# Softcap attention, gated MLP and gated convolution on one core: the product of the values with the reciprocals is issued two ticks later behind the sums

## The chip, the core and the metric

One core of a Trainium2 chip runs the whole program in one launch. The metric is device time in microseconds, the median of the runs shown; lower is better. TensorE (PE in the profile) multiplies matrices, VectorE (DVE) and ScalarE (ACT) work element by element, GpSimd (POOL) clears tiles and issues the DMAs of the normalization, and SyncE (SP) issues the other DMAs.

## The reference

Three stages follow one another. The change lies in the first, the attention with capped scores over 2 batches and 12 heads of 448 positions and 64 columns:

```python
scores = scale * np.matmul(q, k.transpose(0, 1, 3, 2))
scores = cap * np.tanh(scores / cap)
scores = scores - np.max(scores, axis=-1, keepdims=True)
attn = np.exp(scores)
attn = attn / (np.sum(attn, axis=-1, keepdims=True) + 1e-09)
return np.matmul(attn, v)
```

Its output, regrouped to x of 2 x 448 x 768, goes into a gated MLP (a matrix product with w_in, gelu, a layer norm, a product over positions, a gate, w_out and a residual), and that into a gated convolution (w2_in, relu, three taps, sigmoid, w2_out).

## The kernel before

The heads are worked in pairs, twelve of them: pair N belongs to batch N // 6 and to rows N % 6 of X, the tile in which the attention's output stands for the next stage. A loop over R (L452) takes two steps of R per pair, one per half. In an even step, `scores` (L308) issues the twelve products of the first half, in an odd one the nine of the second; ScalarE then takes the tanh of the half (L317) and the exponential (L318), and since the PSUM tile of the scores exists once, the next half's products wait for that tanh. `values` (L344) follows one step behind, from R = 13 on two: products of the exponentials with V into the PSUM tile pv, and products with ones into the PSUM tile su, which are the sums of the softmax. Beside them VectorE prepares K and Q of later pairs (L92, L95, L262, L263) and decodes pieces of the weights w_in (L135 to L152, tile f), and at R = 13, 17, 21, 23 and 25 TensorE gets products of the next stage that read finished rows of X (`FILL`, tile mo).

When both halves of a pair are through, `norm` (L377) copies the sums to se on VectorE (L389), which frees su, and the values to E on ScalarE (L390). Every second pair it normalizes both together. GpSimd sends the sums to a narrow tile ss (L397). Three pieces of work are put off with `later(k, fn)`, which runs fn k ticks on; a step of R has two ticks. `s1` adds a guard to the sums, takes the reciprocal (L406, L407) and has GpSimd send it to DRAM as d (L410). `s1b` has GpSimd send it back, broadcast to all rows, as rb (L416, four DMAs). `s2` multiplies E by rb on VectorE (L423), copies the product to X on ScalarE (L94 in `split`) and puts the rest of it beside it with a subtraction on VectorE (L95). There are six such normalizations: of the pairs 0 and 1, 2 and 3, 4 and 5, 6 and 7, 8 and 9, and of pair 10. `norm` is reached for them at R = 4, 8, 12, 17, 21 and 23, between the two ticks of the step. Pair 11 goes another way, without DMAs (`norm_pe`).

What sets the order: a scheduler places each instruction when it is issued, and `pin(last)` puts an instruction behind a given one. L406 and L423 are pinned behind `lastv`, the last marked instruction on VectorE, which is the end of a preparation of Q or K, of a gelu, or of an `s2` (its subtraction); the copy to X is pinned behind `lasta`, the last exponential. Functions that fall due in one tick run in the order in which they were put off.

Of the kernel before, what the change touches and what calls it, by code (L numbers as in the profile page):

```python
# [48 lines left out]
def stages(  # L49
# [23 lines left out]
    def pin(last):  # L73
        return tc.issue_after(last[0].ins) if last[0] is not None else ExitStack()
# [3 lines left out]
    def later(k, fn):  # L78
        due.setdefault(now[0] + k, []).append(fn)
# [10 lines left out]
    def split(raw, hi, lo, hi_eng="v"):  # L90
        if hi_eng == "v":
            V.tensor_copy(hi, raw)  # L92
        else:
            A.activation(hi, raw, AF.Copy)  # L94
        return V.tensor_tensor(out=lo, in0=raw, in1=f(hi), op=ALU.subtract)  # L95
# [123 lines left out]
    def attention(att, psa):  # L219
# [124 lines left out]
        def values(N, half):  # L344
# [28 lines left out]
            if half:  # L373
                del acc[N]
                norm(N, ps, su)

        def norm(N, ps, su):  # L377
            b, p = divmod(N, NPAIR)
            if N >= B * NPAIR - NFAST:
                return norm_pe(N, ps, su)  # L380

            j = N % 2
            if j == 0:
                pairs[:] = (
                    att.tile([P, 2, S // 2], F32, tag="se", name="se", bufs=2),
                    att.tile([P, 2, S], F32, tag="E", name="E", bufs=3),
                )
            se, e = pairs
            V.tensor_copy(se[:, j], su)  # L389
            A.activation(e[:, j], ps, AF.Copy)  # L390
            last = N == B * NPAIR - NFAST - 1
            if j == 0 and not last:
                return

            m = j + 1
            ss = att.tile([P, 14], F32, tag="ss", name="ss", bufs=2)[:, : 7 * m]
            G.dma_start(ss, se[::32, :m])  # L397
            rb = att.tile([P, 2, S], F32, tag="rb", name="rb", bufs=2)
            eb, rb = e[:, :m], rb[:, :m]

            ds = []


            def s1():
                with pin(lastv):
                    V.tensor_scalar(out=ss, in0=ss, scalar1=guard, scalar2=None, op0=ALU.add)  # L406
                V.reciprocal(out=ss, in_=ss)  # L407
                ds.append(dr.tile([2, 2, m, S // 2], F32, tag=f"d{m}", name="d"))
                d = ds[0]
                G.dma_start(d.rearrange("h f j (p c) -> (h f j p) c", c=7 * m), ss)  # L410

            def s1b():
                (d,) = ds
                for h in range(2):
                    for i in range(m):
                        G.dma_start(  # L416
                            rb[h * D : (h + 1) * D, i].rearrange("p (f c) -> p f c", f=2),
                            d[h, :, i].partition_broadcast(D),
                        )

            def s2():
                with pin(lastv):
                    V.tensor_tensor(out=eb, in0=eb, in1=rb, op=ALU.mult)  # L423
                with pin(lasta):
                    lastv[0] = split(eb, X[:, 0, p - j : p + 1, b], X[:, 1, p - j : p + 1, b], "a")

            later(3, s1)
            later(4, s1b)
            later(11, s2)

        def norm_pe(N, ps, su):

            b, p = divmod(N, NPAIR)
            r = att.tile([P, 2, S // 2], F32, tag="se", name="r", bufs=2)[:, 0]
            V.tensor_scalar(out=r, in0=su, scalar1=guard, scalar2=None, op0=ALU.add)
            V.reciprocal(out=r, in_=r)
            e = att.tile([P, 2, S], F32, tag="E", name="E", bufs=3)[:, 0]
            A.activation(e, ps, AF.Copy)
            rp = psa.tile([P, 512], F32, tag="su", name="rp", bufs=1)[:, :S]
            for c in range(2):  # L440
                for h in range(2):
                    lastr[0] = T.matmul(
                        rp[h * D : (h + 1) * D, c * S // 2 : (c + 1) * S // 2],
                        lhsT=sel[:, 2 * h + c], rhs=r, start=True, stop=True,
                    )
            V.tensor_tensor(out=e, in0=e, in1=rp, op=ALU.mult)
            split(e, X[:, 0, p, b], X[:, 1, p, b], "a")
# [450 lines left out]
```

## Time and profile before

| | us |
|---|---|
| runs shown | 344.87, 345.75, 345.68 |
| median of the runs | 345.68 |
| span of the profiled execution | 344.2 |
| the profiled execution's own time | not given beside its span |
| TensorE busy | 329.7 (96% of the span) |
| VectorE busy | 252.6 (73%) |
| ScalarE busy | 224.9 (65%) |
| GpSimd busy | 35.2 (10%) |

The span goes from the first to the last instruction of one execution; a run's time takes in what lies around it. Times in the rows are microseconds from the start of the span. A bracket at the end of a row gives how long the engine stood idle before it and what ended that idle time. DMA-issuing instructions are not counted as busy.

### The profile page before, as it was taken

Reading aid. Unit: us, or ns where it says so; the run is one execution under the profiler, and the core shown is the slowest. Engines: PE = TensorE matmul, PEld = TensorE weight load, DVE = VectorE, ACT = ScalarE, POOL = GpSimd, SP = SyncE. Lnnn points to the kernel's source line nnn. Section 1 sums busy time; section 2 is a strip of 40 time slices with the busy share of each in tenths; the row PEclk is TensorE's granted clock in tenths of the full one; section 3 lists DMA queues with packets and bytes.
Section 4 is the critical chain, followed back from the end, with each engine's and each line's share of the span. In section 5 each row is a group of like instructions: output and inputs, shape, how many; then the busy total and the mean of one; then the engine's idle time right before and its main releaser. Section 6 shows DMA issues by size and latency. Waiting matters only on the chain.

```text
span 344.2 us, 5129 instructions
## 1 busy us (share of the span) xinstructions
PE 329.7 (96%) x1814; PEld 251.5 (73%) x1814; DVE 252.6 (73%) x493; ACT 224.9 (65%) x361; POOL 35.2 (10%) x71
## 2 busy tenths in 40 slices
PE   6999999979999999999999999999999999999992
PEld 4544444534446567898899999999999999999991
DVE  4487878769686367997999679997995999970000
ACT  1799889978798236585775564465784988863110
POOL 3000300403030323110121000000000000000000
PEclk9899999998999999999999999999999999999997
DMA  6857754854421124313213384002284122013111
GB/s 178 264 165 237 196 158 142 206 140 124 84 68 43 48 90 126 113 46 93 62 62 122 109 256 170 2 0 59 65 274 155 32 61 91 3 54 132 58 55 33
DMA packets 18698, 37.67 MB, mean 109 GB/s; under 512 B 3980, under 2 KB 9160, under 8 KB 18664
## 3 DMA queue, kind: packets, MB, share of 16 engines
q1 hardware_dynamic: 16952, 34.41, 32.3%
q0 software_dynamic: 1472, 2.61, 3.2%
q8 instruction: 16, 0.26, 0.3%
q10 hardware_dynamic: 240, 0.23, 0.3%
q14 instruction: 18, 0.15, 0.1%
HBM read 34.41 MB, written 2.79 MB: 108 GB/s over the span
## 4 chain that ended last, share of the span: by engine, by line
PE 76%; issue 11%; DMA 5%; DVE 3%; POOL 2%; SPq 1%; ACT 0%; DVEq 0%; POOLq 0%; ACTq 0%
PE mo L98 17%; PE mo L99 17%; PE mo L100 17%; PE pv L305 5%; PE sc L305 4%; PE mo L603 3%; PE mo L605 3%; PE mo L604 3%; PE mo L305 3%; PE su L305 2%; DMA d<-ss 2%; DMA rb<-d 2%; POOL rb L416 2%; DMA ss<-se 1%; PE idle L305 1%
## 5 line engine op out<-in xcount | busy, mean ns | idle before, releaser
L98 PE MATMUL mo<-X,WI 128*128 128x448 f32 x126 | 46.1, 367 | 0.0
L99 PE MATMUL mo<-X,WI 128*128 128x448 f32 x126 | 45.9, 366 | 0.0
L100 PE MATMUL mo<-X,WI 128*128 128x448 f32 x126 | 45.9, 365 | 0.0
L305 PE MATMUL pv<-raw,V 128*64 128x448 f32 (+1 forms) x168 | 45.1, 579 | 0.0
L305 PE MATMUL sc<-Q,K 64*128 64x448 f32 (+1 forms) x252 | 39.3, 395 | 5.3 <-ACT raw L317 3.5
L318 ACT ACTIVATE raw<-raw,one 128x1792 f32<-128x1792 f32 (+3 forms) x26 | 39.1, 1503 | 0.6
L305 PEld LDWEIGHTS sc<-Q,K 64*128 64x128 f32 (+1 forms) x252 | 24.5, 188 | 20.2 <-issue 6.7
L130 ACT ACTIVATE f<-f 128x512 f32<-128x512 f32 (+3 forms) x57 | 31.0, 545 | 10.7 <-DMA f<-in_w_out_dram 5.8
L317 ACT ACTIVATE raw<-sc 128x1792 f32<-128x1792 f32 (+1 forms) x22 | 32.4, 1475 | 7.8 <-PE sc L305 7.5
L140 DVE SCALAR_TENSOR_TENSOR f<-f 128x512 uint32<-128x512 uint32 (+3 forms) x57 | 30.3, 542 | 9.0 <-ACT f L133 8.5
L99 PE MATMUL mo<-HG,W 128*128 128x448 f32 x96 | 34.8, 365 | 0.0
L100 PE MATMUL mo<-HG,W 128*128 128x448 f32 x96 | 34.7, 365 | 0.0
L98 PE MATMUL mo<-HG,W 128*128 128x448 f32 x96 | 34.1, 365 | 0.0
L143 DVE SCALAR_TENSOR_TENSOR f<-f 128x512 uint32<-128x512 uint32 (+3 forms) x57 | 30.7, 546 | 0.3
L305 PEld LDWEIGHTS pv<-raw,V 128*64 128x64 f32 (+1 forms) x168 | 11.9, 145 | 22.0 <-issue 18.5
L98 PEld LDWEIGHTS mo<-X,WI 128*128 128x128 f32 x126 | 23.6, 188 | 2.4 <-DVE u L179 0.4
L100 PEld LDWEIGHTS mo<-X,WI 128*128 128x128 f32 x126 | 23.6, 188 | 2.0
L99 PEld LDWEIGHTS mo<-X,WI 128*128 128x128 f32 x126 | 23.7, 188 | 2.0
L783 ACT ACTIVATE o<-mo 128x448 f32<-128x448 f32 x12 | 6.3, 543 | 26.1 <-PE mo L100 23.0
L133 ACT ACTIVATE f<-f 128x256 uint32<-128x256 uint32 (+2 forms) x44 | 22.6, 515 | 0.0
L99 PEld LDWEIGHTS mo<-HG,W 128*128 128x128 f32 x96 | 18.0, 188 | 1.4
L98 PEld LDWEIGHTS mo<-HG,W 128*128 128x128 f32 x96 | 18.0, 188 | 1.4
(141 smaller groups left out, 650.3 us busy)
## 6 DMA issues: line engine op xcount, KB each, us to landing
f<-in_w_in_dram SPq DMA_DIRECT2D x24, 512.0 KB, 4.4
f<-in_w_out_dram SPq DMA_DIRECT2D x24, 256.0 KB, 4.2
V<-in_vL_dram SPq DMA_DIRECT2D x12, 256.0 KB, 3.7
f<-in_w_out_dram SPq DMA_DIRECT2D x8, 384.0 KB, 3.1
qr<-in_qT_dram SPq DMA_DIRECT2D x24, 112.0 KB, 3.1
out_dram<-o SPq DMA_DIRECT2D x12, 224.0 KB, 1.9
rb<-d POOLq DMA_DIRECT2D x22, 112.0 KB, 3.8
kr<-in_kT_dram SPq DMA_DIRECT2D x11, 112.0 KB, 3.1
```

The costliest lines, as they stand in the source:

```text
L98: matmul(ps, lhsT=whi, rhs=xhi, start=start, stop=False)
L99: matmul(ps, lhsT=whi, rhs=xlo, start=False, stop=False)
L100: matmul(ps, lhsT=wlo, rhs=xhi, start=False, stop=stop)
L130: A.activation(f(h), f(h), AF.Copy, scale=2.0**-112)
L133: A.activation(l, l, AF.Copy, scale=0.93 * 2.0**-29)
L140: V.scalar_tensor_tensor(out=l, in0=h, scalar=3, in1=l, op0=ALU.logical_shift_left, op1=ALU.bitwise_or)
L143: V.scalar_tensor_tensor(out=l, in0=h, scalar=0x80000000, in1=l, op0=ALU.bitwise_and, op1=ALU.bitwise_or)
L305: lastm[0] = T.matmul(*args, **kw)
L317: A.activation(raw[:, t], ps[:, t, :S], AF.Tanh, **sc)
L318: lasta[0] = A.activation(raw[:, t], raw[:, t], AF.Exp, scale=capc)
L603: T.matmul(ps, lhsT=xs(0, k), rhs=WI[1][:, 0, k], start=k == 0, stop=False)
L604: T.matmul(ps, lhsT=xs(0, k), rhs=WI[1][:, 1, k], start=False, stop=False)
```

## The change

One number changes, the count of ticks from a normalization's issue to its `s2`:

```diff
             later(3, s1)
             later(4, s1b)
-            later(11, s2)
+            later(13, s2)
```

It moves instructions on VectorE, ScalarE, GpSimd and SP; TensorE's stand as before.

On VectorE, at the first normalization's product (E_282, rb_363) and the second one's sums (ss_525), K0, Q and the decoding of the weights (f64, WI0) around them:

```order
 L95 TENSOR_TENSOR K0_87<-kr0_89,K0_87 128x512
+L406 TENSOR_SCALAR ss_525<-ss_525,one_72 128x14
+L135 TENSOR_SCALAR f64_530<-f64_530 128x512
 L423 TENSOR_TENSOR E_282<-E_282,rb_363 128x896
 L263 SCALAR_TENSOR_TENSOR Q_585<-qr_483,one_72,Q_585 128x448
 L143 SCALAR_TENSOR_TENSOR f64_452<-f64_452 128x512
+L407 RECIPROCAL ss_525<-ss_525 128x14
 L149 CAST WI0_76<-f64_452 128x512
```

The two instructions on ss_525, which stood behind the subtraction of X from E_282 one step later, now stand on both sides of the product.

On ScalarE, at the second normalization's copy to X (E_442), with the tanh and exponential of one half (raw), the decoding (f64) and the copy of the values (pv):

```order
+L130 ACTIVATE f64_696<-f64_696 128x512
+L317 ACTIVATE raw_776<-sc_775 128x1344
+L318 ACTIVATE raw_776<-raw_776,one_72 128x1344
 L94 ACTIVATE X_75<-E_442 128x2x448
-L130 ACTIVATE f64_696<-f64_696 128x512
-L317 ACTIVATE raw_779<-sc_778 128x1344
-L390 ACTIVATE E_806<-pv_762 128x448
-L318 ACTIVATE raw_779<-raw_779,one_72 128x1344
 L130 ACTIVATE f64_724<-f64_724 128x512
+L390 ACTIVATE E_806<-pv_759 128x448
```

The copy to X stands behind the tanh and the exponential of its step, where it stood ahead of them.

On VectorE, at the second normalization's product (E_442, rb_527) and the third one's sums (ss_691):

```order
 L95 TENSOR_TENSOR K0_87<-kr0_89,K0_87 128x512
+L406 TENSOR_SCALAR ss_691<-ss_691,one_72 128x14
+L135 TENSOR_SCALAR f64_696<-f64_696 128x512
+L423 TENSOR_TENSOR E_442<-E_442,rb_527 128x896
 L263 SCALAR_TENSOR_TENSOR Q_750<-qr_649,one_72,Q_750 128x448
-L143 SCALAR_TENSOR_TENSOR f64_618<-f64_618 128x512
-L423 TENSOR_TENSOR E_442<-E_442,rb_527 128x896
-L149 CAST WI1_77<-f64_618 128x512
-L152 TENSOR_TENSOR WI1_77<-f64_618,WI1_77 128x512
+L143 SCALAR_TENSOR_TENSOR f64_615<-f64_615 128x512
+L407 RECIPROCAL ss_691<-ss_691 128x14
```

The product stands two operations earlier on VectorE, and the third normalization's sums stand ahead of it. On GpSimd the four DMAs of the fifth normalization's rb now stand ahead of the sixth one's ss, which they followed.

## Rows read from the trace of the kernel before

**Rows 1.** the page's head: span, and TensorE's busy time with its share.

```profile
span 344.2 us, 5129 instructions
...
PE 329.7 (96%) x1814; PEld 251.5 (73%) x1814; DVE 252.6 (73%) x493; ACT 224.9 (65%) x361; POOL 35.2 (10%) x71
```

**Rows 2.** the page's chain that ended last, shares of the span by engine.

```profile
PE 76%; issue 11%; DMA 5%; DVE 3%; POOL 2%; SPq 1%; ACT 0%; DVEq 0%; POOLq 0%; ACTq 0%
```

**Rows 3.** timeline of PE: start, duration, instructions, [idle before <- releaser].

```profile
57.69 1.48 PE L305 MATMUL sc<-Q,K 64*128 64x448 f32 x12 [0.23 <-ACT raw L317]
...
66.54 1.72 PE L305 MATMUL pv<-raw,V 128*64 128x448 f32 x8
...
68.71 1.69 PE L305 MATMUL sc<-Q,K 64*128 64x448 f32 x9
...
72.18 0.96 PE L305 MATMUL su<-raw,ones 128*32 128x224 f32 x16
75.33 1.50 PE L305 MATMUL sc<-Q,K 64*128 64x448 f32 x12 [2.19 <-ACT raw L317]
76.76 3.09 PE L305 MATMUL pv<-raw,V 128*64 128x448 f32 x8
...
80.57 1.69 PE L305 MATMUL sc<-Q,K 64*128 64x448 f32 x9
...
97.64 0.58 PE L305 MATMUL su<-sm,ones 128*32 128x224 f32 x8 [0.39 <-DVE se L389]
```

**Rows 4.** timeline of ACT, around its longest idle.

```profile
72.60 0.95 ACT L94 ACTIVATE X<-E 128x896 fp32r<-128x896 f32 x1 [2.46 <-DVE E L423]
...
74.02 1.27 ACT L317 ACTIVATE raw<-sc 128x1344 f32<-128x1344 f32 x1
```

**Rows 5.** timeline of DVE, 49 to 79 us.

```profile
49.44 0.69 DVE L95 TENSOR_TENSOR K<-kr,K 128x512 fp32r<-128x512 f32 x1
...
56.78 1.08 DVE L95 TENSOR_TENSOR X<-E,X 128x896 fp32r<-128x896 f32 x1
57.78 0.23 DVE L406 TENSOR_SCALAR ss<-ss,one 128x14 f32<-128x14 f32 x1
...
62.40 0.38 DVE L389 COPY se<-su 128x224 f32<-128x224 f32 x1
...
66.87 0.70 DVE L143 SCALAR_TENSOR_TENSOR f<-f 128x512 uint32<-128x512 uint32 x1
71.47 1.09 DVE L423 TENSOR_TENSOR E<-E,rb 128x896 f32<-128x896 f32 x1 [3.90 <-DMA rb<-d]
...
78.59 0.38 DVE L389 COPY se<-su 128x224 f32<-128x224 f32 x1
```

**Rows 6.** the tile f to 130 us: duration ns min/median/max of L135.

```profile
L135 DVE TENSOR_SCALAR f<-f x13: 178/422/427, 10.1 to 96.3; 128x512 uint32<-128x512 uint32 x12, 128x24 uint32<-128x24 uint32 x1
```

**Rows 7.** timeline of POOL's DMA issues in the same stretch.

```profile
46.48 0.73 POOL L397 DMA_DIRECT2D ss<-se  x1 [5.33 <-DVE se L389]
...
60.32 0.57 POOL L410 DMA_DIRECT2D d<-ss  x1 [13.10 <-DVE ss L407]
...
62.74 2.54 POOL L416 DMA_DIRECT2D rb<-d  x4 [1.86 <-DMA d<-ss]
```

**Rows 8.** landings of ss issued at 46.48 and at 65.27, of rb issued from 62.74.

```profile
DMA to landing us min/median/max: 4.0/4.0/4.0
...
DMA to landing us min/median/max: 6.3/6.3/6.3
...
DMA to landing us min/median/max: 6.0/6.6/6.8
```

**Rows 9.** stretches: busy by engine (instructions), PEclk, DMA share, GB/s.

```profile
60.00:65.00 5.00, 4.80 (x35) 2.81 (x33) 4.31 (x9) 4.77 (x5) 2.82 (x5) 1.00 0.65 174
...
76.76:78.50 1.74, 1.74 (x8) 0.68 (x8) 1.74 (x5) 1.74 (x3) 0.00 (x0) 0.56 0.15 52
...
130.00:150.00 20.00, 20.00 (x93) 17.26 (x93) 17.73 (x35) 13.00 (x27) 5.53 (x6) 1.00 0.34 103
```

## The prediction

> **What bounds the kernel now.** I read the page first: span 344.2 us, TensorE busy 329.7 of it, 96% [rows 1]. Anything that pays must therefore take out one of TensorE's few idle stretches, or a stretch in which it is busy but slow. The chain of waits says where to look: beside 76% TensorE it holds 5% DMA, 3% VectorE and 2% GpSimd [rows 2], and the lines behind these are those of the normalization, L397 to L423. So the next view is TensorE's timeline in the attention stage. The step whose scores begin at 75.33 waits 2.19 us with nothing running, and it waits for ScalarE's tanh, L317 [rows 3]. ScalarE's timeline shows why that tanh is late: the engine stood idle 2.46 us before the copy of X (L94) at 72.60, waiting for VectorE's product L423; only behind that copy comes the tanh at 74.02 [rows 4]. VectorE stood idle 3.90 us before that product, waiting for the broadcast reciprocals rb [rows 5]. GpSimd's issues close the loop: this second normalization's sums went out at 46.48 and landed 4.0 us later [rows 7, 8], but its DMA of the reciprocals, d, left at 60.32 after 13.10 us of waiting for L407 [rows 7], and rb, issued from 62.74, landed up to 6.8 us after its issue [rows 7, 8]. The sums lay ready from 50.5; L406 took them up at 57.78, right behind the subtraction of X at 56.78 of the normalization before [rows 5].
>
> That is an order, not a shortage. A product (s2) and the next normalization's sums (s1), four steps of R apart, fall due in one tick: 2R+1+11 for the one, 2(R+4)+1+3 for the other. The product is taken first and sets lastv to its subtraction, and the sums are then pinned behind it.
>
> **What the change does.** With 13 the product falls due one tick pair later, behind those sums. The first order piece shows it: the sums' L406 (ss_525) moves from behind X's subtraction to before L423, L407 follows three operations later, and L423 itself stays between the same K and Q operations. The sums of the third normalization and of the fifth move ahead in the same way (ss_691 in the third piece); the fourth's keep their place behind the third's product, because five steps lie between them. No instruction is added or removed, TensorE's order is unchanged, and GpSimd's changes at one place, the fifth rb before the sixth ss.
>
> *Second normalization.* VectorE reaches L406 when K's subtraction of 49.44 is through, about 50.0, and now waits for the sums until 46.48 + 4.0 = 50.5: a new wait of 0.4. L423 (1.09), Q and L143 (0.60 to 0.70 each, [rows 5]) and L407 follow, so d leaves near 53.8 instead of 60.32. Keeping the distance from d to rb of the trace, 62.74 - 60.32 = 2.42, and the largest landing, 6.8 after an issue that ends 1.9 later, rb is there by 53.8 + 2.4 + 1.9 + 6.8 = 64.9. Its product now comes at about 67.3 (below). The 3.90 us wait disappears with 2.4 us to spare.
>
> *What TensorE gets.* (a) X's copy of the first normalization stands one exponential later on ScalarE, so the tanh before the scores at 57.69 is no longer behind it: 0.23 us [rows 3]. (b) The second copy moves in the same way behind the tanh and exponential of its step (second order piece), and its product is early anyway. TensorE's sums of 72.18 end 0.96 later; ScalarE's tanh, free from 70.14 (72.60 less the idle 2.46), is done before 72.2. The 2.19 us go. (c) Behind the idle time the eight products at 76.76 took 3.09 us instead of 1.72 at 66.54, at a granted clock of 0.56 of full speed, so mostly at 1.2 GHz [rows 3, 9]. From the eight products to the next nine it is 80.57 - 76.76 = 3.81 against 68.71 - 66.54 = 2.17: 1.64 us, which return if the clock stays up. (d) At 97.64 TensorE waits 0.39 for VectorE's copy of the sums, se, out of PSUM [rows 3]. VectorE was late there from waiting for the third rb, and that wait goes the same way: with its sums taken up at 66.8 (below), d leaves near 70.0 and rb is there by 81.1 at the distances above, while its product stands thirteenth behind the se copy of 75.2, twelve operations between them at 7.12 / 13 = 0.55 us each on average, near 82. Sum: 0.23 + 2.19 + 1.64 + 0.39 = **4.45 us**.
>
> The Trainium skill speaks against (c): TensorE: Matmul & The Clock Gate, "A second HAM failure mode: psum-queue depth-cycling", reports a kernel whose short idles between groups of products were enough for the clock to swing. By that rule the sum is 2.81, since short idles remain. The trace does not bear it out: from 60 to 65 us TensorE was busy 4.80 of 5.00 and the clock stayed at 1.00, which is 2.4 GHz [rows 9]. I take the 1.64.
>
> *What it costs.* VectorE gets no more work, but its work up to the next se copy is put in another order, and that copy is what TensorE's next sums wait for. I bound it by rows. The third normalization's se is copied at 62.40 [rows 5]; GpSimd, no longer issuing rb until 65.28 (62.74 + 2.54, [rows 7]), sends the sums at about 62.8. The landing is not known there; its ends are the 4.0 of 46.48 and the 6.3 of 65.27 [rows 8]. I take 4.0, because the later one shared the queue with four rb that are now gone: 66.8. VectorE could use them at about 66.2, 0.6 before the 66.87 at which L143 stands [rows 5]. So it idles 0.6, and L423 starts at 67.3. From L423 to the se copy the trace has 78.59 - 71.47 = 7.12 without a gap [rows 5]. Operations overlap by some 0.08: the 1.08 of 56.78 is followed after 1.00. So the change takes out X's subtraction (1.00), one L406 (0.23 - 0.08 = 0.15, [rows 5]) and two L135 (0.42 - 0.08 = 0.34 each, [rows 6]), 1.83 in all, and puts in L407, as short as L406 (0.15), and four operations of L143's kind, one on Q, one L140 and two L143 (0.70 - 0.08 = 0.62 each, [rows 5]), 2.63: 7.92 us. The copy runs from 75.2 to 75.6 (0.38 long). TensorE's scores now start at 72.18 + 0.96 - 0.23 = 72.9; the eight products follow 76.76 - 75.33 = 1.43 later and take 1.72, so its next sums come at 76.0 [rows 3]. So the copy is hidden, by 0.4 us. X's subtraction follows at 76.3, while the fill that reads it stands behind those sums and nine scores of 1.69 [rows 3], past 77.6: hidden. On ScalarE the copy L94 (0.95, [rows 4]) now precedes the tanh of the following step and can cost TensorE between nothing and its length there; I take 0.1, since the engine gets the 2.46 us back in which it idled before.
>
> The Trainium skill's page DMA: Bandwidth & Descriptors, "Anatomy of one DMA — SWDGE (gpsimd) path", fits 2.0 us plus a small size term. By it the sums land at 64.8, VectorE does not wait, and the sum stays where it is; by the row of 6.3 the copy comes 2.3 later and 1.9 us of the gain are lost. The landings seen, 4.0 and 6.3, are both above that fit.
>
> Behind 130 us TensorE is busy 20.00 of 20.00 us [rows 9] on the same instructions, so the gain is carried to the end. Total: 4.45 - 0.1 = **4.35 us**. The profiled execution would go from 344.2 to 339.85. The page gives its span alone; the median of the runs, 345.68, lies 1.48 above it, and 345.68 - 4.35 = **341.3 us**.
>
> **Rivals.**
> *The sums land late.* A wait for ss takes the place of the wait for rb. With a landing of 6.3, TensorE loses 1.9, or 3.54 if the clock falls again: 343.2 to 344.9. For it: VectorE has only 0.4 us of cover at that copy. Against: 6.3 was measured behind four rb in flight.
> *The clock falls anyway.* Then (c) stays: 345.68 - 2.71 = 343.0. For it: it fell behind the idle 2.19 [rows 3, 9], and the short idles of ScalarE's making remain. Against: 1.00 over the stretch with 0.20 us idle [rows 9]. (The Trainium skill's page named under (c) is its source.)
> *Slower.* The same place, L406 of the third normalization, now at the head of VectorE's queue, with Q, the decoding of weights and the se copy behind it and TensorE behind that copy. With landing x, TensorE idles x - 4.4, and the clock takes 1.64 more; that outweighs 4.35 from x = 7.1. At 8.3 the kernel is slower by 3.9 + 1.64 - 4.35 = 1.2: 346.9. Against: the longest landing of a small ss is 6.3 and of the large rb 6.8.
> *No change.* The order moves but the gain is given back: ScalarE, busy 4.77 of 5.00 us at 60 [rows 9], could become the bound in place of the wait. Then 345.7. Against: its tanh is free at 72.2 and needed at 72.8.
>
> **Chances.** About 0.3%, 1.0 us, can be told from no change. Forecast 0.74; clock 0.08; sums late 0.08, of which half below 344.6; no change 0.05; slower 0.05. Faster: 0.74 + 0.08 + 0.04 + 0.01 for a small rest of the no-change case = 0.87; same 0.07; slower 0.06. The range reaches from 340.5, the forecast less the 0.8 by which the lowest run, 344.87, lies under the median, to 343.9, which takes in the clock's case and the better half of the late sums; 0.15 lies above, little below.
>
> **What would show it.** Right: L406 of the second normalization near 50.5 and d near 54; no wait of L423 for rb over 0.5 us; no TensorE idle over 0.4 us between 57 and 100; clock 1.00 around the eight products that took 3.09; a span near 339.9. Wrong: L406 idle 2 us or more for ss, an idle of TensorE that ends with se L389, or a clock near 0.5 in the same step.

## The result and the profile after it

The changed kernel takes **342.0 us** (median of 4 runs, 341.23 to 343.89) against 345.35 (344.87 to 345.75, 4 runs) before on the same chip: a ratio of 0.9904, 95% interval 0.9875 to 0.9933. The forecast was 341.3, between 340.5 and 343.9. The profiled execution is the longest of the four, 343.89, with a span of 342.1 us. Of the runs of the kernels below, three count as slow, 407.63 us of split2, 814.2 of ss_sync and 353.97 of fill_su, and are left out of the ratios but not of the medians.

The head of the page and the chain that ended last answer to [rows 1, 2]:

```profile
span 342.1 us, 5132 instructions
...
PE 329.2 (96%) x1814; PEld 252.2 (74%) x1814; DVE 252.9 (74%) x493; ACT 224.9 (66%) x361; POOL 35.8 (10%) x71
...
PE 79%; DMA 7%; DVE 7%; issue 3%; POOL 1%; ACT 0%; SPq 0%; DVEq 0%; ACTq 0%; POOLq 0%
```

The chain's "issue" falls from 11% to 3%: two stretches, of 13.1 and 13.4 us, in which the chain of before stood in GpSimd's queue while it waited for L407, are no longer on it. TensorE's busy time over the whole span is only 0.5 us less; what that hides follows next.

Before anything is compared one thing has to be set aside. Two windows of the start of the changed kernel's profiled execution, and one of the attention stage, answer to [rows 9]:

```profile
12.00:14.00 2.00, 2.00 (x8) 1.34 (x5) 0.00 (x0) 1.32 (x2) 0.00 (x0) 0.50 0.89 140
14.00:16.00 2.00, 2.00 (x11) 0.99 (x11) 0.94 (x2) 0.96 (x2) 0.00 (x0) 0.73 1.06 397
...
60.00:100.00 40.00, 38.73 (x275) 19.14 (x271) 36.06 (x66) 36.64 (x34) 9.37 (x16) 1.00 0.48 132
```

From 12 to 16 us the clock is 0.50 and then 0.73 of full speed; in the execution of before it is 0.97 and 1.00 in the same two windows. This lies far ahead of the first instruction that the change moves; the first sums of sixteen products start at 22.70 instead of 20.92, and the rows stay 1.78 later up to the place of the change, near 50 us. I therefore compare a stage: from the third to the last of the twelve `su<-raw,ones` rows of sixteen products on TensorE's timeline. Before, it runs from 36.81 to 123.23, **86.42 us**:

```profile
36.81 0.96 PE L305 MATMUL su<-raw,ones 128*32 128x224 f32 x16
...
123.23 0.96 PE L305 MATMUL su<-raw,ones 128*32 128x224 f32 x16
```

After, it runs from 38.59 to 121.39, **82.80 us**:

```profile
38.59 0.96 PE L305 MATMUL su<-raw,ones 128*32 128x224 f32 x16
...
121.39 0.96 PE L305 MATMUL su<-raw,ones 128*32 128x224 f32 x16
```

The gain inside it is 3.62 us: TensorE's idle time in the stage falls by 1.86 (3.13 to 1.27) and its busy time by 1.76 (83.29 to 81.53), the products at the low clock. The spans differ by only 2.1, mainly because the start gives back 1.78.

TensorE's timeline of the changed kernel answers to [rows 3]:

```profile
59.16 1.49 PE L305 MATMUL sc<-Q,K 64*128 64x448 f32 x12
...
66.56 1.49 PE L305 MATMUL sc<-Q,K 64*128 64x448 f32 x12 [0.32 <-ACT raw L317]
...
73.61 0.96 PE L305 MATMUL su<-raw,ones 128*32 128x224 f32 x16
74.51 1.50 PE L305 MATMUL sc<-Q,K 64*128 64x448 f32 x12
75.94 1.72 PE L305 MATMUL pv<-raw,V 128*64 128x448 f32 x8
78.49 0.59 PE L305 MATMUL su<-sm,ones 128*32 128x224 f32 x8 [0.83 <-DVE se L389]
...
95.80 0.58 PE L305 MATMUL su<-sm,ones 128*32 128x224 f32 x8
```

The idle times of 0.23, 2.19 and 0.39 are gone, and the eight products that took 3.09 take 1.72, with the clock at 1.00 over the whole of 60 to 100 us. A new idle time of 0.83 stands ahead of the sums at 78.49, and it ends with se, L389, VectorE's copy of the previous sums out of PSUM. VectorE's timeline says why that copy is late; it answers to [rows 5]:

```profile
53.15 0.23 DVE L406 TENSOR_SCALAR ss<-ss,one 128x14 f32<-128x14 f32 x1 [1.25 <-DMA ss<-se]
...
53.64 1.09 DVE L423 TENSOR_TENSOR E<-E,rb 128x896 f32<-128x896 f32 x1
...
69.74 0.23 DVE L406 TENSOR_SCALAR ss<-ss,one 128x14 f32<-128x14 f32 x1 [1.95 <-DMA ss<-se]
...
70.22 1.08 DVE L423 TENSOR_TENSOR E<-E,rb 128x896 f32<-128x896 f32 x1
...
78.05 0.39 DVE L389 COPY se<-su 128x224 f32<-128x224 f32 x1
```

The product at 70.22 no longer waits for rb (3.90 before). In its place the sums' addition L406, now ahead of the product, waits for the DMA that brings the sums: 1.25 and 1.95 us. Behind the second of these waits everything of VectorE's shifts, the se copy with it. GpSimd's issues answer to [rows 7], and the landings of the two ss, issued at 48.26 and 64.52 (a landing is the time from the issue of a DMA until its data have arrived), to [rows 8]:

```profile
48.26 0.73 POOL L397 DMA_DIRECT2D ss<-se  x1 [6.24 <-DVE se L389]
56.38 0.57 POOL L410 DMA_DIRECT2D d<-ss  x1 [7.38 <-DVE ss L407]
59.69 2.37 POOL L416 DMA_DIRECT2D rb<-d  x4 [2.74 <-DMA d<-ss]
64.52 0.75 POOL L397 DMA_DIRECT2D ss<-se  x1 [2.46 <-DVE se L389]
...
DMA to landing us min/median/max: 4.9/4.9/4.9
...
DMA to landing us min/median/max: 5.1/5.1/5.1
```

d of the second normalization leaves at 56.38, which is 54.60 on the clock of before, instead of 60.32.

### The profile page after: what moved, and what is told of

It reads as the page before. It is cut to its first block, busy times and chain, and to the rows that moved or that the text cites. A ratio compares the mean times of both kernels' runs of the same rounds, so it can differ in the third digit from the quotient of the medians.

```text
span 342.1 us, 5132 instructions
## 1 busy us (share of the span) xinstructions
PE 329.2 (96%) x1814; PEld 252.2 (74%) x1814; DVE 252.9 (74%) x493; ACT 224.9 (66%) x361; POOL 35.8 (10%) x71
## 4 chain that ended last, share of the span: by engine, by line
PE 79%; DMA 7%; DVE 7%; issue 3%; POOL 1%; ACT 0%; SPq 0%; DVEq 0%; ACTq 0%; POOLq 0%
PE mo L98 18%; PE mo L99 17%; PE mo L100 17%; PE pv L305 6%; PE sc L305 5%; PE mo L603 3%; PE mo L604 3%; PE mo L605 3%; PE mo L305 3%; PE su L305 3%; DMA kr<-in_kT_dram 2%; DMA ss<-se 2%; DMA qr<-in_qT_dram 2%; PE idle L305 1%; DVE Q L263 1%
## 5 line engine op out<-in xcount | busy, mean ns | idle before, releaser
L305 PE MATMUL pv<-raw,V 128*64 128x448 f32 (+1 forms) x168 | 43.7, 561 | 0.0
L140 DVE SCALAR_TENSOR_TENSOR f<-f 128x512 uint32<-128x512 uint32 (+3 forms) x57 | 30.7, 547 | 9.2 <-ACT f L133 8.7
```

The costliest lines, as they stand in the source:

```text
L140: V.scalar_tensor_tensor(out=l, in0=h, scalar=3, in1=l, op0=ALU.logical_shift_left, op1=ALU.bitwise_or)
L305: lastm[0] = T.matmul(*args, **kw)
```

## The experiments

**Theory:** two things together make the gain. The sums of the second and third normalization, taken up ahead of the product, bring rb in time; and the product's copy to X on ScalarE (L94) stands behind the tanh instead of ahead of it. The 0.8 us short of the forecast are the landing of ss, which VectorE now waits for with the se copy queued behind. **Rivals:** the later product alone makes the gain, or the earlier sums alone; the clock's 1.64 us have another cause than the 2.19 us idle; the 0.83 us have another cause than the landing.

The stage defined above, from the profile of each kernel (one execution each), with TensorE's idle times of 0.2 us and more from 57 to 100 us and the ratio of the times to those of before on the same chip:

| kernel | stage, us | against before | TensorE idle, us (what ends it) | median, us | ratio, 95% interval |
|---|---|---|---|---|---|
| before | 86.42 | | 0.23, 0.32, 2.19 (tanh); 0.39 (se) | 345.35 | |
| the change | 82.80 | -3.62 | 0.32 (tanh); 0.83 (se) | 342.0 | 0.9904, 0.9875 to 0.9933 |
| after_again | 82.38 | -4.04 | 0.32 (tanh); 0.40 (se) | 343.5 | 0.9897, 0.9866 to 0.9929 |
| sums_first | 82.35 | -4.07 | 0.23, 0.34 (tanh); 0.22 (se) | 342.64 | 0.9882, 0.9857 to 0.9908 |
| prod_only | 83.45 | -2.97 | 0.32 (tanh); 1.41, 0.21 (se) | 342.96 | 0.9896, 0.9852 to 0.994 |
| pin_product | 82.07 | -4.35 | 0.22, 0.33 (tanh) | 342.58 | 0.9877, 0.9852 to 0.9903 |
| split2 | 81.85 | -4.57 | 0.32 (tanh) | 342.46 | 0.9891, 0.9857 to 0.9926 |
| ss_sync | 81.81 | -4.61 | 0.32 (tanh) | 343.41 | 0.9889, 0.9837 to 0.9941 |
| fill8 | 89.06 | +2.64 | 0.24, 0.32, 1.50 (tanh); 1.83 (se) | 349.02 | 1.0057, 1.0026 to 1.0088 |
| fill_su | 90.20 | +3.78 | 0.23, 0.32 (tanh); 1.83, 2.09 (se) | 349.76 | 1.0092, 1.0054 to 1.0129 |

The medians of the seven faster kernels cannot be told apart, since the start of the program moves a time by a microsecond or two from one execution to the next. The stage tells more, but it is one execution per kernel: the changed kernel's two executions differ by 0.42, so a difference of that size between two kernels shows nothing by itself, and the idle times have to carry the argument. after_again, sums_first, pin_product and split2 ran on one chip (before: 346.38), prod_only, fill8 and ss_sync on another (346.8), fill_su on a third (346.3).

### The change once more

The changed kernel without an edit.

> The changed kernel once more, beside the variants. If the gain is what the trace of the change shows between TensorE's sums at 50.70 and those at 121.39 (70.69 us, against 74.31 between 48.92 and 123.23 before), it is 3.6 us faster than before. If the start of the program made up part of the difference, less than 3 or more than 4.5.

The ratio gives 3.6 us, as expected; the difference of the medians, 2.9, is just under the 3 that were to speak for the start. The stage, which leaves the start out, is 4.04 shorter, so the gain is not the start's. The profiled execution has the same picture with smaller numbers: L406 idles 1.30 and 1.52, the landings are 4.9 and 4.6, and TensorE's idle before the sums is 0.40. So the 0.83 is not a constant: with the second landing 0.5 shorter, TensorE waited 0.43 less, and the stage took 0.42 less.

### Only the sums ahead of the product

```diff
-    def later(k, fn):
-        due.setdefault(now[0] + k, []).append(fn)
+    def later(k, fn, first=False):
+        due.setdefault(now[0] + k, []).insert(0 if first else len(due.get(now[0] + k, [])), fn)
...
-            later(3, s1)
+            later(3, s1, True)
```

The product stays due at 11, as before; within a tick the sums come first.

> The product stays at 11 ticks; only within a tick the sums now run before the product. Theory (the sums were pinned behind the product's subtraction, and that is the whole cause): the second normalization's d leaves near 54 to 56, the product waits for rb less than 0.5 us, TensorE's 2.19 us and the 1.64 us of low clock go. X's copy on ScalarE stays ahead of the tanh (0.23 us not gained), and X's subtraction stands ahead of se (1.0 us more in front of TensorE's sums, beside the 0.83 us of the change): 2 to 3 us faster than before. Rival (the gain comes from the product and the copy of X being issued later): no gain, within 0.5 us of before.

The stage is 4.07 shorter than before, as much as with the change (4.04 in its second execution), so the sums ahead of the product are enough. It is also more than the 2 to 3 us expected. L406 idled 1.09 instead of 1.95, with a landing of 4.4. And the subtraction ahead of se cost about 0.5 instead of 1.0: the copy came 8.37 us behind the product, against 7.83 with the change. ScalarE's timeline of this kernel shows how the tanh comes in time:

```profile
72.38 0.93 ACT L94 ACTIVATE X<-E 128x896 fp32r<-128x896 f32 x1
...
73.79 1.27 ACT L317 ACTIVATE raw<-sc 128x1344 f32<-128x1344 f32 x1
```

The copy to X still stands ahead of the tanh, as in [rows 4], but it no longer waits, since rb is there in time. What is not gained is the 0.23 before the scores of the first place: it is there in this kernel and in pin_product (0.23 and 0.22), which both leave the copy to X where it was, and absent in the change, prod_only and split2, which move the copy. That 0.23 belongs to the copy's place, as step (a) had it.

### Only the product later

```diff
-            later(3, s1)
-            later(4, s1b)
-            later(11, s2)
+            later(5, s1)
+            later(6, s1b)
+            later(13, s2)
```

Sums and product both come one tick pair later, so the sums stand behind the subtraction again.

> The change, with the sums' addition moved on as well (two tick pairs for product and sums alike), so that the product is later and the sums stand behind the subtraction of the normalization before, as in the kernel before. Theory, the gain comes from the sums standing ahead of the product: d of the second normalization leaves behind the subtraction of X one step later, at about 66 to 68, rb lands at about 76 to 79, the product L423 waits for it again, 2 to 4 us, and TensorE is late again at one or two places: the stage from the third sums of halves to the last takes about what it takes before, 86.4, within 1.5 us, and the time is within 1.5 us of before. Rival, it is the later product that gains: the stage takes 82 to 83 and the time is as with the change, 3 us or more below before.

The theory had expected no gain, and the stage is 2.97 shorter: it falls in this form. VectorE's and ScalarE's timelines of this kernel:

```profile
59.99 1.09 DVE L95 TENSOR_TENSOR X<-E,X 128x896 fp32r<-128x896 f32 x1
60.99 0.23 DVE L406 TENSOR_SCALAR ss<-ss,one 128x14 f32<-128x14 f32 x1
...
71.85 1.09 DVE L423 TENSOR_TENSOR E<-E,rb 128x896 f32<-128x896 f32 x1 [2.57 <-DMA rb<-d]
...
77.30 0.38 DVE L389 COPY se<-su 128x224 f32<-128x224 f32 x1
```

```profile
70.73 1.26 ACT L317 ACTIVATE raw<-sc 128x1344 f32<-128x1344 f32 x1
72.03 1.42 ACT L318 ACTIVATE raw<-raw,one 128x1344 f32<-128x1344 f32 x1
73.35 0.94 ACT L94 ACTIVATE X<-E 128x896 fp32r<-128x896 f32 x1
```

The order is as expected, but the sums come at 60.99 and not at 64 or later, so d leaves at 62.00 and the product waits 2.57. Now the wait hurts only VectorE: the copy to X has the tanh and the exponential ahead of it on ScalarE, and the tanh is through at 72.0. TensorE's scores do not wait at 73.18. What the late rb still costs is the se copy, 1.41 us of TensorE. So **either half of the change takes out the 2.19 us idle by itself**: the sums in front by making rb early, the later product by letting the tanh pass. The sums in front save more, because they also free the se copy from the wait for rb.

### The product ahead of the wait for the sums

```diff
-    lasta, lastv, lastr = [None], [None], [None]
+    lasta, lastv, lastr, lastp = [None], [None], [None], [None]
...
-                with pin(lastv):
+                with pin(lastp if lastp[0] is not None else lastv):
                     V.tensor_scalar(out=ss, in0=ss, scalar1=guard, scalar2=None, op0=ALU.add)
...
-                    V.tensor_tensor(out=eb, in0=eb, in1=rb, op=ALU.mult)
+                    lastp[0] = V.tensor_tensor(out=eb, in0=eb, in1=rb, op=ALU.mult)
```

The product is due at 11; the sums are pinned behind the product instead of behind its subtraction, so VectorE works on the product while the sums are on their way.

> The product stays at 11 ticks and the sums are pinned behind the product itself, no longer behind its subtraction. Theory: as sums_first, but VectorE's wait for ss (1.25 and 1.95 us in the change) now stands behind the product and is about 1.0 us shorter: 3 to 4 us faster than before. Rival: no gain.

The stage is 4.35 shorter (3 to 4 us were expected), and L406 of the third normalization has no idle time. And the same edit, with the copy to X and the subtraction at 13 and the product staying at 11:

```diff
...
             def s2():
                 with pin(lastv):
-                    V.tensor_tensor(out=eb, in0=eb, in1=rb, op=ALU.mult)
+                    lastp[0] = V.tensor_tensor(out=eb, in0=eb, in1=rb, op=ALU.mult)
+
+            def s2b():
                 with pin(lasta):
...
             later(11, s2)
+            later(13, s2b)
```

> The product stays at 11 ticks with the sums pinned behind it, and its copy and subtraction into X run at 13 ticks. Theory (the gain lost in the change is VectorE's wait for ss in front of se): L406 of the third normalization idles about 1 us instead of 1.95, se is copied about 1 us earlier, TensorE's 0.83 us at the sums and the 0.18 us at the next go: 4.2 to 4.7 us faster than before, 0.6 to 1.0 faster than the change. Rival (those 0.83 us are bounded by something else, K or Q or ScalarE): same as the change.

VectorE's timeline of split2:

```profile
66.97 1.08 DVE L423 TENSOR_TENSOR E<-E,rb 128x896 f32<-128x896 f32 x1
67.98 0.22 DVE L406 TENSOR_SCALAR ss<-ss,one 128x14 f32<-128x14 f32 x1
...
75.33 0.38 DVE L389 COPY se<-su 128x224 f32<-128x224 f32 x1
```

The two ss landed in 4.7 and 3.9 us here, but neither of the two L406 has any idle time, where about 1 us was expected, since the product fills the wait. No idle time of TensorE ends with se any more, and the stage is 4.57 shorter than before, 0.95 and 0.53 shorter than with the change in its two executions. pin_product keeps the 0.22 of the first place. This settles the 0.83: with 1.95, 1.52 and no idle time of this L406, TensorE waits 0.83, 0.40 and not at all for se. It was the wait for the sums.

### The sums by another queue

```diff
-            G.dma_start(ss, se[::32, :m])
+            nc.sync.dma_start(ss, se[::32, :m])
```

> The change, with the sums' small DMA (7 KB) issued by SP between its loads instead of by GpSimd, nothing else edited. It asks what makes up its landing of 4.9 and 5.1 us. Theory, the load on the DMA engines at that moment (a w_in piece of 512 KB and a V of 256 KB go out beside it): it lands 4 us or more after its issue from SP too, L406 of the third normalization is idle 1 us or more, and the stage takes 82 to 83.5 as with the change. Rival, GpSimd's way of issuing sets it: it lands within 3 us, L406 is idle under 0.5, the stall of TensorE ahead of its sums (0.83) is gone, and the stage takes about 81.9, as with the variants that wait for no sums. Third possibility: SP, which takes its DMAs in order, waits for the copy of the sums and its loads of K, Q and V come late: TensorE idles for K or Q, and the time is longer than with the change.

Neither number was met. SP issued the sums at 49.98 and 65.18, and L406, which waited for them, began at 53.41 and 68.95, at most 3.4 and 3.8 us later: less than 4, more than 3. The two L406:

```profile
53.41 0.23 DVE L406 TENSOR_SCALAR ss<-ss,one 128x14 f32<-128x14 f32 x1 [0.70 <-DMA ss<-se]
...
68.95 0.23 DVE L406 TENSOR_SCALAR ss<-ss,one 128x14 f32<-128x14 f32 x1 [0.34 <-DMA ss<-se]
```

The outcome is the rival's: no idle time of TensorE ends with se, and the stage takes 81.81. SP's loads were not late. What share of the landing GpSimd's way of issuing has, and what share the load, stays open. The changed kernel's other landings say something on the load. Windows over the time of the two slow ones, and over two later ones that landed in 2.4 and 2.3 us (the last two columns are the DMA share, which is the mean busy share of the core's DMA engines, and GB/s):

```profile
48.26:53.15 4.89, 4.89 (x37) 2.35 (x35) 3.00 (x6) 4.18 (x5) 0.73 (x1) 1.00 0.60 181
64.52:69.74 5.22, 4.90 (x33) 2.90 (x35) 3.00 (x6) 5.07 (x5) 0.75 (x1) 1.00 0.69 202
88.08:90.50 2.42, 2.42 (x21) 1.17 (x13) 2.35 (x4) 1.95 (x2) 0.74 (x1) 1.00 0.10 4
102.81:105.20 2.39, 2.39 (x21) 0.83 (x18) 2.18 (x5) 1.74 (x2) 0.75 (x1) 1.00 0.25 59
```

These four are 7 KB each by the same queue, and they take twice as long in the windows where the DMA engines are 0.60 to 0.69 busy. Yet the share alone does not decide: the first ss, issued at 32.38, landed in 3.1 us at a share of 0.68. Over the nine executions that send ss from GpSimd, the landings go better with the moment at which the 512 KB of f leave SP. Where f left within 0.6 us of ss, ss landed in 3.9 to 5.3 us (14 landings); where f left 1.0 to 1.1 us ahead, in 3.1 to 4.0 (10); right behind four rb, in 5.4 to 6.5 (3); and from 85 us on, with no f in the 2 us ahead, in 2.2 to 3.3 (27). No run moved f alone, so this goes together but is not shown to be the cause.

### The clock by itself

Both kernels are the one of before with products of zeros more on TensorE, the late rb left in place.

```diff
-        lastm = [None]
+        lastm, lastps = [None], [None]
...
+            lastps[0] = ps
...
+            if R == 15:
+                for _ in range(8):
+                    ordered(lastps[0][:, 3, :S], lhsT=wz[:, :P], rhs=wz, start=True, stop=True)
```

> The kernel before, with eight products of zeros more on TensorE, written to the fourth bank of the scores that nothing reads there, just ahead of the scores that wait 2.19 us for the tanh at 75.33. Everything else is as before, the late rb included. Theory, the clock fell because TensorE stood idle there: the eight products behind these scores (3.09 us before) take about 1.72, the granted clock stays near 1.00, the scores themselves start no earlier, and the stage from the third sums of halves to the last takes 1.4 to 1.8 less than the 86.4 of before, the time 1 to 2 less. Rival, the clock falls there for another reason, or the extra products cost as much as they save: the eight products take 2.5 us or more, and stage and time are within 0.5 us of before or longer.

The eight products missed their place. Their row shows them waiting for the same tanh, then running for 1.89 us in front of the scores:

```profile
75.48 1.89 PE L305 MATMUL sc<-wz 128*128 128x448 f32 x8 [1.50 <-ACT raw L317]
77.43 1.49 PE L305 MATMUL sc<-Q,K 64*128 64x448 f32 x12
```

An idle time of 1.50 stayed in front of them, so the wait was not filled, and the run says little of its question. The second form writes behind the sums, to columns of their bank that no tanh reads:

```diff
-                    psa.tile([P, 512], F32, tag="su", name="su", bufs=1)[:, : S // 2],
+                    psa.tile([P, 512], F32, tag="su", name="su", bufs=1),
...
-            ps, su = acc[N]
+            ps, su = acc[N][0], acc[N][1][:, : S // 2]
...
-                del acc[N]
+                [ordered(acc[6][1][:, 224:], lhsT=wz[:, :P], rhs=wz[:, :288], start=True, stop=True) for _ in range(16 * (N == 6))]
```

> The kernel before, with sixteen products of zeros (288 columns each) more on TensorE right behind the sums of 72.18, written to the free columns of the sums' bank, which no tanh reads: unlike in the run with eight of them they should run while the next scores wait for the tanh. The late rb and the late tanh stay. Theory, the clock fell because TensorE stood idle for 2.19: of that idle time a few tenths are left, the scores start where they did (2.2 behind the end of the sums), the eight products behind them take 1.72 instead of 3.09, and the distance from the sums of 72.18 to the next sums of the same kind, 13.08 before (85.26), is 11.4. A stall that follows it is not counted here. Rival, the clock falls there for another reason: the eight products take 2.5 or more and the distance stays at about 13.1.

TensorE's timeline of this kernel:

```profile
73.25 0.96 PE L305 MATMUL su<-raw,ones 128*32 128x224 f32 x16
74.15 2.37 PE L305 MATMUL su<-wz 128*128 128x288 f32 x16
76.70 1.48 PE L305 MATMUL sc<-Q,K 64*128 64x448 f32 x12 [0.18 <-ACT raw L317]
78.11 1.72 PE L305 MATMUL pv<-raw,V 128*64 128x448 f32 x8
81.66 0.59 PE L305 MATMUL su<-sm,ones 128*32 128x224 f32 x8 [1.83 <-DVE se L389]
...
92.98 0.58 PE L305 MATMUL su<-sm,ones 128*32 128x224 f32 x8 [2.09 <-DVE se L389]
...
95.58 3.02 PE L305 MATMUL pv<-raw,V 128*64 128x448 f32 x6
```

Here they fill the idle time down to 0.18, the scores start 76.70 - 73.25 = 3.45 behind the sums (3.15 before, so 0.30 later), and the eight products take 1.72 with everything else as late as before. From sums to sums it is 13.62; less the 1.83 of the stall behind them and the 0.30, 11.49, where 11.4 was expected. From 78.11 to 79.85, over those eight products, the clock is 1.00 (0.56 before). The clock fell in the kernel before because TensorE stood idle there.

And yet this kernel is slower than before by 0.9%, and fill8 by 0.6%. In fill_su the stall of 1.83 has two parts. L407 and two L140, 1.29 us together, stand ahead of the se copy on VectorE, where they stood behind it before; the scheduler moved them. The other 0.54 are there without that: the wait for rb (4.06 here) holds up the copy as before, and with its products fast again TensorE reaches its next sums before the copy is through. So by this estimate some 1.1 of the clock's 1.64 us could be had at this place alone; the rest needs a VectorE that does not wait for rb.

Most of what fill_su loses, 3.71 of 3.78 us, lies behind that, between its sums of 86.87 and those of 98.53 (11.66 us, against 93.21 - 85.26 = 7.95 before). The 2.09 us at 92.98 stand ahead of sums that did not wait before (89.22). There the se copy came ahead of the third product on VectorE (86.76, the product at 89.69); in fill_su the scheduler put it behind that product (92.55 and 90.94), which waits 3.36 us for rb. The products that follow run at a low clock (3.02 instead of 1.92). fill8 has the same stall, 1.83 us at 91.57, with the same two instructions in the same order.

## Why the prediction was right

**The bound and the order.** Right. The idle time was an order of instructions and not a shortage: over the span VectorE and ScalarE are as busy as before (252.9 and 224.9 us), TensorE runs the same 1814 products, and the stage is 3.62 shorter.

**(a) 0.23, (b) 2.19, (d) 0.39.** All three gone, as forecast. For (b) the prediction named two reasons, the copy behind the tanh and the early rb; sums_first and prod_only show that each is enough alone. That also explains why this forecast was safe: both halves had to fail for the idle time to stay.

**(c) 1.64.** Right: the products take 1.72 at a clock of 1.00, and fill_su shows the cause by itself. The rule cited against it (the Trainium skill, TensorE: Matmul & The Clock Gate, "A second HAM failure mode: psum-queue depth-cycling") is not borne out: idle times of 0.32 and 0.83 were left between 60 and 100 us, and the clock stayed at 1.00.

**The cost: the step that was mis-sized.** "The landing is not known there; its ends are the 4.0 of 46.48 and the 6.3 of 65.27. I take 4.0, because the later one shared the queue with four rb that are now gone." The four rb had landed by about 65.4 (3.2 to 3.9 us after issues that begin between 59.69 and 61.5), one microsecond into the time of the ss of 64.52, and it still took 5.1. The rest of that step's working holds. VectorE takes 78.05 - 69.74 = 8.31 from L406 to the se copy, where the forecast has 75.2 - 66.8 = 8.4. GpSimd sends the sums 9.09 ahead of TensorE's sums of 73.61, where the forecast has 62.8 - 71.95 = -9.15. Only L406 stands 1.28 later than forecast against those same sums, and 1.22 of that is the landing (69.74 - 64.52 = 5.22 to the start of L406, against 4.0). The cover of 0.4 was used up, and 1.28 - 0.4 = 0.88 were due on TensorE; 0.83 were measured. The copy L94 ahead of a tanh, put at 0.1, cost nothing that TensorE's rows show. The sum with the measured landing is 4.45 - 0.83 = 3.62, the gain of the stage. That it fits to the hundredth is luck: the place of (a) gave 0.35 instead of 0.23 (61.00 - 52.71 before, 62.43 - 54.49 after, from sums of sixteen to sums of sixteen), that of (d) 0.46 instead of 0.39 (102.84 - 93.21 and 101.00 - 91.83), and 0.18 that the forecast did not have went at the next wait for se, ahead of the sums of 87.84. The landing of the second normalization's ss was mis-sized as well, 4.9 instead of the 4.0 of its own row, and L406 idled 1.25 there instead of 0.4; no idle time of TensorE followed from it.

The reason for choosing 4.0 was the weak place: it excluded one load (rb) and did not look at the others. V (256 KB) and f of w_in (512 KB) leave SP at 63.77 and 64.41, right ahead of the ss of 64.52. The trace of before has them at 62.10 and 62.75, where the forecast puts its ss, 62.8. In all executions, landings of 3.9 to 5.3 us go with an f that leaves so close to ss; that it is the reason is not shown. Nor were 4.0 and 6.3 the ends: the trace of before holds six landings of ss, 3.6, 4.0, 6.3, 2.8, 2.4 and 3.1 us. By the Trainium skill, DMA: Bandwidth & Descriptors, "Anatomy of one DMA — SWDGE (gpsimd) path", such a small transfer takes 2.0 us and a little; the changed kernel's landings of 2.4 and 2.3 at a DMA share of 0.10 and 0.25 come near it, those of 3.1 at 0.68, 4.9 at 0.60 and 5.1 at 0.69 don't.

**The rivals.** "The sums land late" happened in a mild form, at 5.1 instead of 6.3, and by its own formula (x - 4.4) costs 0.7: one of the signs named for being wrong, an idle time of TensorE that ends with se L389, did appear, though small, and L406 idles 1.95 where 2 was named. The same formula decides for the slower case from 7.1; the longest landing of ss in all these kernels is 6.5, in fill_su. "The clock falls anyway" and "no change" did not occur. Of the signs of being right, d (54.6 on the clock of before, 54 forecast), the product without a wait for rb and the clock of 1.00 came, and L406 came at 51.4 instead of 50.5. Two did not come: TensorE idled 0.83 where no more than 0.4 was named, and the span is 342.1 instead of 339.9, 1.78 of it from the start.

**The median.** 342.0 against the forecast 341.3: 345.35 - 342.0 = 3.35 gained instead of 4.35. The 0.73 that the stage lacks is the landing, less the 0.1 of the copy; the rest lies within what the start of the program moves from run to run.

## What to carry to other kernels

When two pieces of work for one engine fall due in the same moment, put the one that starts a long chain on other engines and queues ahead of the one that only ends a chain, and put work that is ready between the issue of a transfer and the instruction that waits for it. split2 does both: the sums stand ahead of the copy and the subtraction of X, the ready product stands ahead of the sums, and a landing of 4.7 us costs TensorE nothing. Price a new wait on a small DMA by the whole range of its landings in the trace and by what else leaves at that moment, not by one of them. And when an idle time also costs clock, ask whether the time saved by the clock has another late engine right behind it; in fill_su it had, and by the estimate above a third of the 1.64 us was lost to it at that place.

## What the hardware showed that I had not expected

- A DMA of 7 KB took 2.4 and 2.3 us to land at a DMA share of 0.10 and 0.25, 4.9 and 5.1 at 0.60 and 0.69, and 3.1 at 0.68, in one execution of the change, by one queue.
- The length of an idle time alone did not tell whether the clock fell. In fill_su it stayed at 1.00 over 80 to 85 us behind an idle time of 1.83, and was 0.71 from 95 to 100 behind one of 2.09; in fill8 it fell behind 1.83 (the six products after it took 3.21 instead of 1.92) and stayed behind 1.50. The windows of fill_su that show it:

```profile
80.00:85.00 5.00, 3.34 (x23) 2.25 (x23) 5.00 (x12) 3.41 (x3) 2.66 (x5) 1.00 0.44 116
...
95.00:100.00 5.00, 5.00 (x30) 1.80 (x31) 5.00 (x11) 2.66 (x3) 0.00 (x0) 0.71 0.08 27
```

- The start of the program takes a different time from execution to execution: in the ten executions kept, the first sums of sixteen products begin between 20.92 (before) and 24.34 us (after_again). Of the 1.78 between before and the change, 0.33 are a later first product (7.55 against 7.22); in the rest TensorE's products run longer, in a stretch at low clock that lasts to about 15 us instead of about 12. In after_again it is another stall: the clock is 1.00 from 8 to 16 us, TensorE then idles 2.05 us for VectorE's sm, and the clock is 0.55 from 16 to 20.
